# Convolution stage: the inverse transform in three tiles of 120 rows, one more rounded sequence, and a finer order of steps

## The chip, the cores and the metric

The kernel runs on one core of one Trainium2 chip. The metric is device time in microseconds, from one launch; the kernel before takes 2923.79 us (median of 3 runs, 2923.07 to 2927.09).

## What is computed

The reference chains three layers over 2 sequences of 12480 positions and 128 channels. This change touches the first one alone:

```
h_filt = (maximum(pos_emb @ w1, 0) @ w2) * window
Uf = rfft(x * v, n=2 * S);  Hf = rfft(h_filt, n=2 * S)
y = irfft(Uf * Hf, n=2 * S)[:, :S]
out = x * y
```

Two feed-forward layers follow: 128 to 2048 to 128, first with an ELU, then with h * cos(h).

## The kernel before, in words

The program has three stages. First the filter taps are made (lines 203 to 308). Then the convolution runs (lines 310 to 477). Last come the two feed-forward layers (from line 480), which this change leaves alone; they read the convolution's result `xt_d` from DRAM.

The convolution is a Fourier transform written as matmuls. A position is split into a (98 rows) and b (128 columns), and the transform has 90 frequencies along a (`NF`) and 128 along b (`NB`). The 128 channels go in 32 chunks of 4 (`DC` = 4, `NCH` = 32). Each chunk has three inputs: the data sequences k = 0 and k = 1, and the filter taps, k = 2. These are the steps for a chunk c:

- `prod` (line 318): u = x * v on POOL. Each chunk's x and v come in by two DMAs of SP (`load`, line 193).
- Stage A, `st_a` (line 335), for k = 0, 1, 2: the transform over a in plain fp32 into the PSUM tile `ps_a`, 4 matmuls of 180 columns. DVE multiplies by the twiddles (`za`, `zb`, line 345), POOL adds (`z_t`, line 348). For k = 2 ACT also makes the rounded copy `zh` and POOL the remainder `zl` (line 359).
- Stage B, `st_b` (line 362): the transform over b into `ps_b`, 360 columns (4 channels of 90). For k = 0 and 1 it is 4 matmuls in fp32. For k = 2 it is 12 matmuls in the rounded type fp32r: high times high, low times high, high times low. For k = 2 ACT copies the result out as `hr` and `hi_f` (lines 381 to 383). For k = 0 and 1 DVE multiplies by those (`ya` and in place in `ps_b`, lines 389 and 390) and adds (`y_t`, line 392); ACT rounds (`yh`), POOL takes the remainder (`yl`, line 332).
- Stage C, `st_c` (line 397), k = 0 and 1: the inverse over b into `ps_c`. The rows are one channel's 90 frequencies; for each of 4 channels there are 6 rounded matmuls of 256 columns, 24 in all. DVE multiplies by twiddles (`wa`, `wb`, line 412, 90 x 1024), POOL adds (`w_t`, line 419).
- Stage D, `st_d` (line 422), k = 0 and 1: the inverse over a into `ps_d`, 2 fp32 matmuls of 512 columns. DVE multiplies by x (`at`, line 428), SP writes the result to `xt_d` (line 429).

`ps_a`, `ps_b`, `ps_c` and `ps_d` have one buffer each. So a stage may write its tile again only when DVE or ACT has emptied it.

Between these steps the weights of the feed-forward layers are decoded from double words, in small pieces (`top` and `low`, lines 457 to 461; the DVE rows `size`, `mag`, `pw` and the POOL rows `lf`, `full`, `lo` belong to it).

The order is written by hand. The schedule is manual, so each engine runs its instructions in the order in which the Python code emits them. The tuple `steps` (line 465) holds one period: each entry is a whole stage with the number of chunks that it lags and its k. It is run 34 times (line 469).

Of the kernel before, what the change touches and what calls it, by code (L numbers as in the profile page):

```python
# [19 lines left out]
NA = 98  # L20
NB = 128
# [7 lines left out]
NCH = D // DC  # L29
T = 480  # L30
# [22 lines left out]
def tables():  # L53
# [27 lines left out]
def hyena_moe_kernel(ctx: ExitStack, tc: tile.TileContext, x, v, pe, w1, w2,  # L81
# [92 lines left out]
    with tc.manual_schedule():  # L174
        nc.vector.memset(below, BELOW)
        with ExitStack() as cs:
# [4 lines left out]
            ti_t = const.tile([NF, 2, 4 * NB], F32, name="ti_t")  # L181
# [128 lines left out]
            with ExitStack() as vs:  # L310
# [5 lines left out]
                us, zz, yy, hh, ww = {}, {}, {}, {}, {}  # L316

                def prod(c, k):
                    if c < NCH:
                        us[c, k] = p2.tile([NA, DC, NB], F32, name="u_t")  # L320
                        nc.gpsimd.tensor_tensor(us[c, k], xs[c][:, k], vv[c][:, k], op=ALU.mult)
# [7 lines left out]
                def lo_y(c, k):  # L329
                    y, yh = yy[c, k]  # L330
                    yl = p2.tile([NB, 2, DC * NF], F32R, name="yl")
                    nc.gpsimd.tensor_tensor(yl, y, yh.bitcast(F32), op=ALU.subtract)
                    yy[c, k] = (yh, yl)

                def st_a(c, k):
                    ps = pa.tile([NB, 2, 512], F32, name="ps_a")
# [4 lines left out]
                    n = 4 * NF  # L341
                    t1 = p2.tile([NB, 2 * n], F32, name="za")
                    t2 = p2.tile([NB, 2 * n], F32, name="zb")
                    for q, t in ((0, t1), (1, t2)):
                        nc.vector.tensor_tensor(bank2(t), ps[:, :, 0:n],  # L345
                                                tw_t[:, q:q + 1].to_broadcast([NB, 2, n]), op=ALU.mult)
                    z = p2.tile([NB, 2, DC * NF], F32, name="z_t")
                    nc.gpsimd.tensor_tensor(z.rearrange("p r (s k) -> p r s k", s=DC),  # L348
                                            parts(t1, NF), parts(t2, NF)[:, ::-1], op=ALU.add)
                    if k == 2:  # L350
                        zh = skewed(p1, [NB, 2, DC * NF], F32R, SKEW, name="zh")
                        copy_r(zh, z)
# [9 lines left out]
                def st_b(c, k):  # L362
                    ps = pa.tile([NB, 2, 512], F32, name="ps_b")
# [4 lines left out]
                    for r in range(2):  # L368
                        for j, (sl, q) in enumerate(prs[r]):
                            if k == 2:  # L370
                                zh, zl = z
                                mm = ((dft_h, zh), (dft_l, zh), (dft_h, zl))
                            else:
                                mm = ((dft_t, z),)
                            for i, (a, b) in enumerate(mm):
                                nc.tensor.matmul(ps[:, r, 0:n], a[:, sl], b[:, q], start=j == 0 and i == 0,  # L376
                                                 stop=j == 1 and i == len(mm) - 1)
# [15 lines left out]
                    yh = skewed(p2, [NB, 2, n], F32R, SKEW, name="yh")  # L393
                    copy_r(yh, y)
                    yy[c, k] = (y, yh)

                def st_c(c, k):
                    yh, yl = yy.pop((c, k))
                    last = c == NCH - 1
                    ps = pa.tile([NF, 2, 512], F32, name="ps_c", tag="ps_a" if last and k else "ps_c")  # L400
                    n = 2 * NB
                    for s in range(DC):
                        sl = slice(s * NF, (s + 1) * NF)
                        o = ps[:, s // 2, (s % 2) * n:(s % 2 + 1) * n]
                        mm = [(yt[:, r, sl], th[:, (1 - r) * NB:(3 - r) * NB])
                              for r in range(2) for yt, th in ((yh, dft_h), (yh, dft_l), (yl, dft_h))]
                        for j, (a, b) in enumerate(mm):
                            nc.tensor.matmul(o, a, b, start=j == 0, stop=j == 5)  # L408
                    t1 = p1.tile([NF, DC * n], F32, name="wa")
                    t2 = skewed(p1, [NF, DC * n], F32, SKEW, name="wb")  # L410
                    for q, t in ((0, t1), (1, t2)):
                        nc.vector.tensor_tensor(bank2(t), ps, ti_t[:, q:q + 1].to_broadcast([NF, 2, 512]), op=ALU.mult)
                    w = p2.tile([NF, 2, DC, NB], F32, name="w_t")
                    p, q = parts(t1, NB), parts(t2, NB)[:, ::-1]
                    if last:
                        nc.gpsimd.tensor_tensor(w[:, 0], p[:, 0], q[:, 0], op=ALU.add)
                        nc.vector.tensor_tensor(w[:, 1], p[:, 1], q[:, 1], op=ALU.add)
                    else:
                        nc.gpsimd.tensor_tensor(w, p, q, op=ALU.add)
                    ww[c, k] = w  # L420

                def st_d(c, k):
                    w = ww.pop((c, k))
                    ps = pd.tile([NA, DC, NB], F32, name="ps_d")
                    for r in range(2):
                        nc.tensor.matmul(ps, g_t[:, r * NA:(r + 1) * NA], w[:, r], start=r == 0, stop=r == 1)  # L426
                    at = p2.tile([NA, DC, NB], F32, name="at")
                    nc.vector.tensor_tensor(at, ps, xs[c][:, k], op=ALU.mult)
# [26 lines left out]
                bits, rest = bits_of_all(), parts_of_all()  # L455

                def low(c, k):
                    next(rest, None)

                def top(c, k):  # L460
                    next(bits, None)

                next(bits)
                prod(0, 0)
                steps = ((st_b, 1, 0), (prod, 0, 1), (top, 0, 0), (lo_y, 1, 0), (low, 0, 0), (top, 0, 1), (st_a, 0, 2),
                         (st_c, 2, 1), (top, 0, 2), (lo_z, 0, 2), (low, 0, 1), (st_b, 1, 1), (st_a, 0, 0), (lo_y, 1, 1),
                         (st_d, 2, 0), (low, 0, 2), (st_c, 1, 0), (prod, -1, 0), (st_b, 0, 2), (st_a, 0, 1), (top, 0, 3),
                         (st_d, 2, 1))
                for p in range(NCH + 2):
                    for f, back, k in steps:  # L470
                        if 0 <= p - back < NCH or f in (top, low):
                            f(p - back, k)
                    load(p + 2)
# [223 lines left out]
```

## Time and profile before

| | |
|---|---|
| median of 3 runs | 2923.79 us |
| profiled execution, first to last instruction | 2922.3 us |
| PE busy over the span | 2888.7 us (99%) |
| POOL busy | 2632.8 us (90%) |
| DVE busy | 2497.0 us (85%) |
| ACT busy | 2146.6 us (73%) |

The page gives no time for the profiled execution other than its span; the span is 1.5 us below the median of the runs. The trace is read here in microseconds from the span's first instruction. The convolution stage runs from about 51 to 692. "PE" is the matmul itself and "PEld" the load of its stationary operand, which goes on beside it. A matmul's recorded duration includes its way through the array and overlaps the next one, so lengths on PE are taken from start to start. An fp32 matmul is two PE instructions in the trace, a rounded one is one. "SPq" and "ACTq" are DMA issues on those queues.

### The profile page before, as it was taken

Reading aid. Unit: us, or ns where it says so; the run is one execution under the profiler, and the core shown is the slowest. Engines: PE = TensorE matmul, PEld = TensorE weight load, DVE = VectorE, ACT = ScalarE, POOL = GpSimd, SP = SyncE. Lnnn points to the kernel's source line nnn. Section 1 sums busy time; section 2 is a strip of 40 time slices with the busy share of each in tenths; the row PEclk is TensorE's granted clock in tenths of the full one; section 3 lists DMA queues with packets and bytes.
Section 4 is the critical chain, followed back from the end, with each engine's and each line's share of the span. In section 5 each row is a group of like instructions: output and inputs, shape, how many; then the busy total and the mean of one; then the engine's idle time right before and its main releaser. Section 6 shows DMA issues by size and latency. Waiting matters only on the chain.

```text
span 2922.3 us, 40341 instructions
## 1 busy us (share of the span) xinstructions
PE 2888.7 (99%) x13580; PEld 2393.3 (82%) x13580; DVE 2497.0 (85%) x3241; ACT 2146.6 (73%) x3332; POOL 2632.8 (90%) x1908
## 2 busy tenths in 40 slices
PE   8999999998999999999999999999999999999999
PEld 6878787886888888888888887888888888888887
DVE  5888888887998998899899998888888888888887
ACT  3322323224988898888888888888888888888887
POOL 4888888886999999999999998999999999999998
PEclk9999999998999999999999999999999999999999
DMA  3333333333000000000000001000000000000000
GB/s 105 90 81 88 97 89 86 88 83 97 14 11 14 11 12 14 14 11 11 14 11 14 11 11 60 11 14 11 14 11 14 11 11 14 11 14 11 13 12 14
DMA packets 83104, 96.82 MB, mean 33 GB/s; under 512 B 6106, under 2 KB 68088, under 8 KB 82898
## 3 DMA queue, kind: packets, MB, share of 16 engines
q1 hardware_dynamic: 77072, 88.20, 10.6%
q10 hardware_dynamic: 5826, 6.04, 0.7%
q8 instruction: 109, 1.79, 0.3%
q14 instruction: 97, 0.79, 0.1%
HBM read 59.94 MB, written 34.28 MB: 32 GB/s over the span
## 4 chain that ended last, share of the span: by engine, by line
PE 92%; ACT 3%; DVE 2%; issue 2%; POOL 1%; DMA 0%; ACTq 0%; POOLq 0%; DVEq 0%
PE h_ps L545 35%; PE o_ps L614 34%; PE ps_b L376 8%; PE ps_c L408 6%; PE ps_a L340 4%; PE ps_d L426 4%; ACT e L582 1%; DVE e L575 1%; DVE e L584 1%; ACT e L573 1%; PE h_ps L277 1%; ACT gh L97 1%; ACT ot L622 1%; PE w_ps L218 0%; PE r_ps L259 0%
## 5 line engine op out<-in xcount | busy, mean ns | idle before, releaser
L106 POOL TENSOR_TENSOR gl<-e,gh 128x960 fp32r<-128x960 f32 x780 | 1463.7, 1888 | 88.6 <-ACT gh L97 45.3
L545 PE MATMUL h_ps<-xh,w 128*128 128x480 f32 x3328 | 1022.3, 388 | 15.5 <-DVE e L562 5.5
L614 PE MATMUL o_ps<-gh,w 128*128 128x480 f32 x3120 | 933.0, 380 | 0.0
L545 PEld LDWEIGHTS h_ps<-xh,w 128*128 128x128 f32 x3328 | 623.0, 189 | 150.5 <-issue 26.6
L614 PEld LDWEIGHTS o_ps<-gh,w 128*128 128x128 f32 x3120 | 586.8, 188 | 92.9 <-POOL gh L105 0.2
L575 DVE SCALAR_TENSOR_TENSOR e<-e,h_ps 128x960 f32<-128x960 int32 x416 | 479.9, 1154 | 193.1 <-ACT e L573 67.0
L545 PE MATMUL h_ps<-xl,w 128*128 128x480 f32 x1664 | 634.6, 381 | 0.0
L560 DVE SCALAR_TENSOR_TENSOR e<-e,t_ps 128x480 f32<-128x480 f32 x832 | 539.6, 652 | 108.8 <-ACT t_ps L558 87.7
L614 PE MATMUL o_ps<-gl,w 128*128 128x480 f32 x1560 | 594.3, 381 | 2.0 <-POOL gl L106 2.0
L556 ACT ACTIVATE e<-h_ps 128x480 f32<-128x480 f32 x832 | 475.5, 572 | 141.6 <-PE h_ps L545 106.9
L573 ACT ACTIVATE e<-h_ps 128x960 int32<-128x960 f32 x416 | 404.1, 971 | 149.8 <-PE h_ps L545 148.0
L105 POOL TENSOR_SCALAR gh<-e 128x960 fp32r<-128x960 f32 x468 | 466.8, 998 | 42.1 <-DVE e L562 24.1
L558 ACT ACTIVATE t_ps<-h_ps 128x480 f32<-128x480 f32 x832 | 479.4, 576 | 0.0
L562 DVE SCALAR_TENSOR_TENSOR e<-e,h_ps 128x480 f32<-128x480 f32 x780 | 472.3, 647 | 0.0
L582 ACT ACTIVATE e<-e,half_pi 128x960 f32<-128x960 f32 x416 | 453.9, 1091 | 0.3 <-DVE e L575 0.3
L584 DVE TENSOR_TENSOR e<-e,h_ps 128x960 f32<-128x960 f32 x390 | 447.2, 1147 | 1.3 <-ACT e L582 1.2
L545 PEld LDWEIGHTS h_ps<-xl,w 128*128 128x128 f32 x1664 | 314.3, 189 | 52.3 <-POOL xl L106 0.6
L614 PEld LDWEIGHTS o_ps<-gl,w 128*128 128x128 f32 x1560 | 293.7, 188 | 50.6 <-POOL gl L106 3.2
L97 ACT ACTIVATE gh<-e 128x960 fp32r<-128x960 f32 x312 | 312.4, 1001 | 0.0
L376 PE MATMUL ps_b<-z_t,dft_t 128*128 128x360 f32 x512 | 165.7, 466 | 2.1 <-DVE y_t L392 1.7
L348 POOL TENSOR_TENSOR z_t<-za,zb 128x720 f32<-128x720 f32 x96 | 141.1, 1470 | 26.3 <-DVE zb L345 26.3
L408 PE MATMUL ps_c<-dft_h,yh 128*90 128x256 f32 x512 | 160.4, 313 | 0.0
(90 smaller groups left out, 3066.7 us busy)
## 6 DMA issues: line engine op xcount, KB each, us to landing
x_t<-in_x SPq DMA_DIRECT2D x32, 392.0 KB
v_t<-in_v SPq DMA_DIRECT2D x32, 392.0 KB
xt_d<-at SPq DMA_DIRECT2D x64, 196.0 KB
out<-ot SPq DMA_DIRECT2D x52, 240.0 KB
x_in<-xt_d SPq DMA_DIRECT2D x50, 240.0 KB
raw<-in_wi SPq DMA_DIRECT2D x16, 256.0 KB
w_d<-hi SPq DMA_DIRECT2D x32, 128.0 KB
w_d<-lo SPq DMA_DIRECT2D x32, 128.0 KB
```

The costliest lines, as they stand in the source:

```text
L105: ENG[plan[0]].tensor_scalar(hi, full, 1.0, 0.0, op0=ALU.mult, op1=ALU.add)
L106: ENG[plan[1]].tensor_tensor(lo, full, hi.bitcast(F32), op=ALU.subtract)
L545: nc.tensor.matmul(h[:, 0:T], a, b, start=k == 0, stop=k == 2)
L556: nc.scalar.activation(u[:, e], hs[e][:, 0:T], AF.Exp)
L558: nc.scalar.activation(ts[e][:, 0:T], hs[e][:, 0:T], AF.Tanh, scale=0.5)
L560: nc.vector.scalar_tensor_tensor(u[:, e], u[:, e], 1.0, ts[e][:, 0:T], op0=ALU.add, op1=ALU.mult)
L562: nc.vector.scalar_tensor_tensor(gt[:, e], u[:, e], 0.0, hs[e][:, 0:T], op0=ALU.min, op1=ALU.max)
L573: nc.scalar.activation(kq, hv, AF.Copy, scale=1.0 / TWO_PI, bias=0.25)
L575: nc.vector.scalar_tensor_tensor(rr, kq, -TWO_PI, hv, op0=ALU.mult, op1=ALU.add)
L582: nc.scalar.activation(rr, rr, AF.Sin, bias=half_pi)
L584: nc.vector.tensor_tensor(gt, rr, hv, op=ALU.mult)
L614: nc.tensor.matmul(o, a, b[:, e], start=f == 0 and k == 0, stop=f == NFT - 1 and k == len(mm) - 1)
```

## The change

**Three tiles.** Stage C now works on 3 tiles of 120 rows (`NM` = 120, `NT` = 3), each with the 90 frequencies of one channel and 30 frequencies of the fourth. For that, DVE's add that writes `y_t` stores its columns in another order and is two instructions, one for three channels and one for the fourth. DVE's two multiplies and POOL's add behind stage C have 120 x 768 elements in place of 90 x 1024. Stage D needs the fourth channel on 90 rows again: three DMAs on SP's queue move 30 rows each from `w_t` to a new tile `v_w`. Stage D is then 2 matmuls of 384 columns from `w_t` and 2 of 128 columns from `v_w`.

**Rounded passes.** Stage B for k = 1 takes the rounded form that k = 2 has: ACT makes `zh`, POOL makes `zl`, and 12 rounded matmuls replace 4 in fp32. In both, the 8 products that need only `zh` are emitted ahead of the 4 that need `zl`.

**Order.** The stages are cut into steps (matmuls, evacuation, add, rounding), and a new list of 44 steps is one period. The filter's stage A runs one chunk ahead, and stage B follows stage A within the period. The loads of x and v are issued at the end of the period, as before. The table `ti_t` grows from 90 x 1024 to 120 x 1536 words.

```diff
+NT = 3
+NM = DC * NF // NT
...
+                    if len(z) == 1:
+                        groups = (((dft_t, z[0]),),)
+                    else:
+                        groups = (((dft_h, z[0]), (dft_l, z[0])), ((dft_h, z[1]),))
...
-                nc.vector.tensor_tensor(y, t1, pv[:, ::-1], op=ALU.add)
...
+                    for o, a, b, e in ((slice(0, NF), 0, m, NT), (slice(NF, NM), m, n, NT)):
+                        nc.vector.tensor_tensor(yv[:, :, :, o], t1[:, :, a:b].rearrange("p r (i k) -> p r i k", i=e),
+                                                q[:, :, a:b].rearrange("p r (i k) -> p r i k", i=e), op=ALU.add)
...
-                    for s in range(DC):
-                        sl = slice(s * NF, (s + 1) * NF)
-                        o = ps[:, s // 2, (s % 2) * n:(s % 2 + 1) * n]
+                    for i in range(NT):
+                        sl = slice(i * NM, (i + 1) * NM)
...
+                    v = p2.tile([NF, 2, NB], F32, name="v_w")
+                    m = NM - NF
+                    for i in range(NT):
+                        nc.sync.dma_start(v[i * m:(i + 1) * m], w[NF:NM, i])
+                    ww[c, k] = (w, v)
...
+                    for o, rhs in ((ps[:, 0:NT], w[0:NF]), (ps[:, NT:DC], v.rearrange("p (i r) b -> p i r b", i=1))):
+                        for r in range(2):
+                            nc.tensor.matmul(o, g_t[:, r * NA:(r + 1) * NA], rhs[:, :, r], start=r == 0, stop=r == 1)
...
-                steps = ((st_b, 1, 0), (prod, 0, 1), (top, 0, 0), (lo_y, 1, 0), (low, 0, 0), (top, 0, 1), (st_a, 0, 2),
...
-                for p in range(NCH + 2):
...
+                steps = """
+                    t c21 l10 A00 D20 a00 y11 C10 A01 w21 L02 Y11 z00 d20 B02 t a01 o c10 o u-10
+                    D21 o z01 l11 h02 w10 t t B00 A-12 d21 y00 H01 u-11 C11 L01 B01 Y00 a-12 z-12
+                    x-20 H-12
+""".split()
```

In the new list a capital A, B, C or D is a stage's matmuls, the small letter its evacuation (h and y for stage B), z and w POOL's adds, H and Y the roundings on ACT, L and l the remainders on POOL, t and o the decoding, u the product, x the loads. The first number is the lag in chunks, the last digit is k. So PE's order in a period is A00 D20 C10 A01 B02 D21 B00 A-12 C11 B01.

On PE, in the middle of a period, before the change: the end of the filter's stage B, then stages A, D, B, A and the start of C.

```order
L376 MATMUL ps_b<-zl,dft_h 128x360
L340 MATMUL ps_a<-fa_t,u_t 128x180 x4
L426 MATMUL ps_d<-w_t,g_t 98x512 x2
L376 MATMUL ps_b<-z_t,dft_t 128x360 x4
L340 MATMUL ps_a<-fa_t,h_all 128x180 x4
L408 MATMUL ps_c<-dft_h,yh 90x256
```

And with the change:

```order
L385 MATMUL ps_b<-zl_1401,dft_h 128x360 x4
L463 MATMUL ps_d<-w_t,g_t 98x384 x2
L463 MATMUL ps_d<-v_w,g_t 98x128 x2
L385 MATMUL ps_b<-z_t,dft_t 128x360 x4
L342 MATMUL ps_a<-fa_t,h_all 128x180 x4
L432 MATMUL ps_c<-dft_h,yh 120x256
```

Stage A for a data sequence no longer stands between the filter's stage B and stage D, and stage D ends with two matmuls that read the moved rows.

On DVE, around the step that empties `ps_b`, before the change:

```order
L428 TENSOR_TENSOR at<-ps_d,x_t 98x512
L389 TENSOR_TENSOR ya<-ps_b,hr 128x720
L390 TENSOR_TENSOR ps_b<-ps_b,hi_f 128x2x360
L392 TENSOR_TENSOR y_t<-ya,ps_b 128x720
L139 TENSOR_SCALAR size<-ps_w 128x256
L143 SCALAR_TENSOR_TENSOR ps_w<-ps_w,size 128x256
L345 TENSOR_TENSOR za<-ps_a,tw_t 128x720
L345 TENSOR_TENSOR zb<-ps_a,tw_t 128x720
L412 TENSOR_TENSOR wa<-ps_c,ti_t 90x1024
L412 TENSOR_TENSOR wb<-ps_c,ti_t 90x1024
```

And with the change:

```order
L467 TENSOR_TENSOR at<-ps_d,x_t 98x512
L402 TENSOR_TENSOR ya<-ps_b,hr 128x720
L403 TENSOR_TENSOR ps_b<-ps_b,hi_f 128x2x360
L408 TENSOR_TENSOR y_t<-ya,ps_b 128x6x90
L408 TENSOR_TENSOR y_t<-ya,ps_b 128x6x30
L349 TENSOR_TENSOR za<-ps_a,tw_t 128x720
L349 TENSOR_TENSOR zb<-ps_a,tw_t 128x720
L144 TENSOR_SCALAR size<-ps_w 128x256
L440 TENSOR_TENSOR wa<-ps_c,ti_t 120x768
L440 TENSOR_TENSOR wb<-ps_c,ti_t 120x768
```

The add is two instructions, and the filter's `za`, `zb` stand directly behind it.

On SP's queue, one period before the change:

```order
L429 DMA xt_d<-at 98x4x128
L164 DMA w_d<-hi 128x256
L120 DMA raw<-in_wo 128x2x128
L429 DMA xt_d<-at 98x4x128
L198 DMA x_t<-in_x 98x2x512
L199 DMA v_t<-in_v 98x2x512
L170 DMA w_d<-lo 128x256
```

And with the change:

```order
L455 DMA v_w<-w_t 30x256 x3
L468 DMA xt_d<-at 98x4x128
L175 DMA w_d<-lo 128x256
L169 DMA w_d<-hi 128x256
L455 DMA v_w<-w_t 30x256 x3
L125 DMA raw<-in_wo 128x2x128
L468 DMA xt_d<-at 98x4x128
L203 DMA x_t<-in_x 98x2x512
L204 DMA v_t<-in_v 98x2x512
```

Seven DMAs a period become thirteen; the first three copies now stand behind the previous period's loads of x and v, the other three ahead of this period's.

## Rows read from the trace of the kernel before

**Rows 1.** The page: its first line, and busy time with share of the span.

```profile
span 2922.3 us, 40341 instructions
PE 2888.7 (99%) x13580; PEld 2393.3 (82%) x13580; DVE 2497.0 (85%) x3241; ACT 2146.6 (73%) x3332; POOL 2632.8 (90%) x1908
```

**Rows 2.** By stretch: length, busy PE, PEld, DVE, ACT, POOL, clock, DMA share, GB/s.

```profile
317.44:650.47 333.03, 333.03 (x1837) 266.59 (x1836) 293.94 (x374) 99.42 (x204) 279.66 (x222) 1.00 0.33 89
650.00:700.00 50.00, 44.28 (x219) 31.94 (x217) 33.54 (x41) 7.63 (x15) 27.84 (x23) 0.91 0.41 125
...
324.00:326.00 2.00, 2.00 (x12) 1.47 (x11) 2.00 (x3) 1.14 (x2) 1.65 (x2) 1.00 0.00 0
```

**Rows 3.** The page: the chain of waits that ended last, by engine.

```profile
PE 92%; ACT 3%; DVE 2%; issue 2%; POOL 1%; DMA 0%; ACTq 0%; POOLq 0%; DVEq 0%
```

**Rows 4.** Timeline of PE, one period, then 17 periods on: start, duration, instructions.

```profile
301.91 2.58 PE L376 MATMUL ps_b<-z_t,dft_t 128*128 128x360 f32 x8
304.33 1.39 PE L340 MATMUL ps_a<-fa_t,u_t 98*128 98x180 f32 x8
305.55 1.88 PE L426 MATMUL ps_d<-w_t,g_t 90*98 90x512 f32 x4
...
310.09 0.33 PE L376 MATMUL ps_b<-zh,dft_h 128*128 128x360 f32 x1
...
312.08 1.38 PE L340 MATMUL ps_a<-fa_t,u_t 98*128 98x180 f32 x8
313.30 1.88 PE L426 MATMUL ps_d<-w_t,g_t 90*98 90x512 f32 x4
315.02 2.59 PE L376 MATMUL ps_b<-z_t,dft_t 128*128 128x360 f32 x8
317.44 1.39 PE L340 MATMUL ps_a<-fa_t,h_all 98*128 98x180 f32 x8
...
321.49 1.37 PE L376 MATMUL ps_b<-z_t,dft_t 128*128 128x360 f32 x4
...
650.47 1.39 PE L340 MATMUL ps_a<-fa_t,h_all 98*128 98x180 f32 x8
```

**Rows 5.** Timeline of PEld in the filter stage: two loads of 128 columns.

```profile
41.78 0.30 PEld L259 LDWEIGHTS r_ps<-pe_t,w_t 128*128 128x128 f32 x2
```

**Rows 6.** Groups by line and form, 100 to 650 us: count, busy us, mean ns.

```profile
L348 POOL TENSOR_TENSOR z_t<-za,zb 128x720 f32<-128x720 f32 x85 | 124.9, 1470 | 16.8 <-DVE zb L345 16.8
L419 POOL TENSOR_TENSOR w_t<-wa,wb 90x1024 f32<-90x1024 f32 x57 | 113.7, 1995 | 10.0 <-DVE wb L412 10.0
...
L376 PEld LDWEIGHTS ps_b<-z_t,dft_t 128*128 128x128 f32 x454 | 84.2, 190 | 52.7 <-issue 14.1
...
L345 DVE TENSOR_TENSOR zb<-ps_a,tw_t 128x720 f32<-128x720 f32 x84 | 75.4, 897 | 0.0
L412 DVE TENSOR_TENSOR wb<-ps_c,ti_t 90x1024 f32<-90x1024 f32 x56 | 67.8, 1210 | 0.0
L359 POOL TENSOR_TENSOR zl<-z_t,zh 128x720 fp32r<-128x720 f32 x28 | 40.7, 1455 | 0.0
L428 DVE TENSOR_TENSOR at<-ps_d,x_t 98x512 f32<-98x512 f32 x57 | 38.7, 679 | 0.0
```

**Rows 7.** Timeline of DVE in that period: the steps that empty `ps_b`.

```profile
317.70 0.91 DVE L389 TENSOR_TENSOR ya<-ps_b,hr 128x720 f32<-128x720 f32 x1 [1.55 <-issue]
...
319.46 0.90 DVE L392 TENSOR_TENSOR y_t<-ya,ps_b 128x720 f32<-128x720 f32 x1
```

**Rows 8.** Timeline of ACT in that period: the last copy out of `ps_b`.

```profile
313.00 0.48 ACT L383 ACTIVATE hi_f<-ps_b 128x360 f32<-128x360 f32 x1
```

**Rows 9.** Timeline of DMA issues: x of a chunk, and a read-back with its reader.

```profile
316.56 0.84 SPq L198 DMA_DIRECT2D x_t<-in_x  x1
...
691.05 0.34 ACTq L523 DMA_DIRECT2D x_in<-xt_d  x1
...
693.76 0.59 POOL L105 TENSOR_SCALAR xh<-x_in 128x480 fp32r<-128x480 f32 x1 [4.77 <-DMA x_in<-xt_d]
```

More of the change, by code (lines that the diff above doesn't have):

```diff
@@ L315, in hyena_moe_kernel @@
                 bank = vs.enter_context(tc.tile_pool(name="bank", bufs=1, space=PSUM))
[L316 to L321, printed above, removed]
+                us, pas, za_, zz, pbs, hh, yy, pcs, wab, ww, pds = ({} for _ in range(11))
+                PS = {"a": "ps_a", "b": "ps_b", "c": "ps_c"}
                 def bank2(t):
@@ L346, in st_a, with add_z @@
                                                 tw_t[:, q:q + 1].to_broadcast([NB, 2, n]), op=ALU.mult)
+                    za_[c, k] = t1, t2
+                def add_z(c, k, at):
+                    t1, t2 = za_.pop((c, k))
                     z = p2.tile([NB, 2, DC * NF], F32, name="z_t")
@@ L367, in st_b @@
                     z = zz.pop((c, k))
[L368 to L377, printed above, removed]
@@ new lines, in mm_b, with out_h @@
+                    for i, group in enumerate(groups):
+                        for r in range(2):
+                            mm = [(a[:, sl], b[:, q]) for sl, q in prs[r] for a, b in group]
+                            for j, (a, b) in enumerate(mm):
+                                nc.tensor.matmul(ps[:, r, 0:n], a, b, start=i == j == 0,
+                                                 stop=i == len(groups) - 1 and j == len(mm) - 1)
+                def out_h(c, k, at):
+                    ps, n = pbs.pop((c, k)), DC * NF
+                    hr = p2.tile([NB, 1, n], F32, name="hr")
+                    hi = p2.tile([NB, 2, n], F32, name="hi_f")
+                    nc.scalar.activation(hr[:, 0], ps[:, 0, 0:n], AF.Copy)
+                    nc.scalar.activation(hi[:, 0], ps[:, 1, 0:n], AF.Copy)
+                    nc.scalar.activation(hi[:, 1], ps[:, 1, 0:n], AF.Copy, scale=-1.0)
+                    hh[c] = (hr, hi)
@@ L386, in st_b, with mul_y @@
+                def mul_y(c, k, at):
                     hr, hi = hh[c]
+                    ps, n = pbs.pop((c, k)), DC * NF
                     t1 = p1.tile([NB, 2, n], F32, name="ya")
@@ L414, in st_c, with out_c @@
-                    p, q = parts(t1, NB), parts(t2, NB)[:, ::-1]
-                    if last:
+                            nc.tensor.matmul(ps[:, i * n:(i + 1) * n], a, b, start=j == 0, stop=j == 5)
+                    pcs[c, k] = ps
+                def out_c(c, k, at):
+                    ps, n = pcs.pop((c, k)), NT * 2 * NB
+                    t1 = p1.tile([NM, n], F32, name="wa")
+                    t2 = skewed(p1, [NM, n], F32, SKEW, name="wb")
+                    for q, t in ((0, t1), (1, t2)):
+                        nc.vector.tensor_tensor(t, ps[:, 0:n], ti_t[:, q], op=ALU.mult)
+                    wab[c, k] = t1, t2
@@ L416, in st_c, with add_w @@
+                def add_w(c, k, at):
+                    p, q = (t.rearrange("p (i r k) -> p i r k", i=NT, r=2) for t in wab.pop((c, k)))
+                    q = q[:, :, ::-1]
+                    w = p2.tile([NM, NT, 2, NB], F32, name="w_t")
+                    if c == NCH - 1:
                         nc.gpsimd.tensor_tensor(w[:, 0], p[:, 0], q[:, 0], op=ALU.add)
-                        nc.vector.tensor_tensor(w[:, 1], p[:, 1], q[:, 1], op=ALU.add)
+                        nc.vector.tensor_tensor(w[:, 1:NT], p[:, 1:NT], q[:, 1:NT], op=ALU.add)
@@ L418, in st_c @@
                     else:
                         nc.gpsimd.tensor_tensor(w, p, q, op=ALU.add)
[L420 to L426, printed above, removed]
+                    v = p2.tile([NF, 2, NB], F32, name="v_w")
+                    m = NM - NF
@@ L455, in hyena_moe_kernel, with low, top, fetch @@
                 bits, rest = bits_of_all(), parts_of_all()
-                def low(c, k):
+                next(bits)
+                def low(c, k, at):
                     next(rest, None)
-                def top(c, k):
+                def top(c, k, at):
                     next(bits, None)
-                next(bits)
-                prod(0, 0)
-                steps = ((st_b, 1, 0), (prod, 0, 1), (top, 0, 0), (lo_y, 1, 0), (low, 0, 0), (top, 0, 1), (st_a, 0, 2),
-                         (st_c, 2, 1), (top, 0, 2), (lo_z, 0, 2), (low, 0, 1), (st_b, 1, 1), (st_a, 0, 0), (lo_y, 1, 1),
-                         (st_d, 2, 0), (low, 0, 2), (st_c, 1, 0), (prod, -1, 0), (st_b, 0, 2), (st_a, 0, 1), (top, 0, 3),
-                         (st_d, 2, 1))
-                for p in range(NCH + 2):
[L470 to L473, printed above, removed]
+                def fetch(c, k, at):
+                    if c not in xs:
+                        load(c)
+                FN = dict(u=prod, A=mm_a, a=out_a, z=add_z, H=hi_z, L=lo_z, B=mm_b, h=out_h, y=mul_y, Y=hi_y, l=lo_y,
+                          C=mm_c, c=out_c, w=add_w, D=mm_d, d=out_d, t=top, o=low, x=fetch)
+                def step(name, c, k, at=""):
+                    if name in "to" or 0 <= c < NCH:
+                        FN[name](c, k, at)
+                steps = """
[3 more added lines that the diff above has]
+""".split()
+                back = lambda s: (s[0], int(s[1:-1]) if len(s) > 1 else 0, int(s[-1]) if len(s) > 1 else 0)
+                for p in range(-2, NCH + 4):
+                    for f, b, k in map(back, steps):
+                        if f in "to" and not 0 <= p < NCH + 2:
+                            continue
+                        step(f, p - b, k)
                 for _ in bits:
```

85 lines of the change are left out of this document (44 added, 41 removed).

## The prediction

> **What bounds the kernel now.** I began with the page's busy times: PE is busy 99% of 2922.3 us, POOL 90%, DVE 85% [rows 1]. A mean over stages says little about one stage, so I cut out 17 whole periods of the convolution, 317.44 to 650.47 [rows 2]. There PE is busy all of 333.03 us at full clock (1.00), and the others are not: per period DVE works 293.94 / 17 = 17.29 us, POOL 279.66 / 17 = 16.45, ACT 5.85. The chain of waits agrees: 92% of it lies on PE [rows 3].
>
> A busy PE may still hide gaps, since its durations overlap. So I read one period start to start [rows 4]: stage B in fp32 2.42 (301.91 to 304.33, again from 315.02), stage A 1.22, stage D 1.72 (313.30 to 315.02), the rounded stage B 1.99 (310.09 to 312.08). Stage C is what is left: 310.09 - 305.55 - 1.72 = 2.82, and 321.49 - 317.44 - 1.22 = 2.83. The sum is 2 x 2.42 + 3 x 1.22 + 2 x 1.72 + 1.99 + 2.82 + 2.83 = 19.58. The period itself is 333.03 / 17 = 19.59. Nothing is left between the stages: PE's own work sets the pace, and an engine beside it costs nothing until it takes longer than PE.
>
> **Part by part, per period.**
>
> *Stage C.* 24 matmuls take 2.82, or 0.118 each. With 18 of the same 256 columns it is 2.12, twice a period: -1.41. The loads grow from 90 to 120 columns; two loads of 128 columns stand 0.30 - 0.19 = 0.11 apart [rows 5, 6], so one still fits under its matmul. The bound on the bad side is stage A's pace, 1.22 / 8 = 0.152 with loads of 128 columns: 18 x 0.152 = 2.74, a gain of 0.16 in all. I take 0.118, as the load row is the nearer one.
>
> *Stage B, k = 1.* 2.42 in fp32 becomes the 1.99 that the rounded one shows [rows 4]: -0.43. The Trainium skill (FP8 and Floating Point Precision, TensorE Precision Notes) says that true fp32 makes 4 passes through the array; taken alone that makes three passes an estimated 1.82, a gain of 0.60, and the forecast 5 us lower. The rows differ from it: a rounded matmul of 360 columns takes 1.99 / 12 = 0.166, a quarter of an fp32 one 2.42 / 16 = 0.151. The measured gain stands.
>
> *Stage D.* The columns stay 512, split 384 and 128. An instruction of 512 takes 1.72 / 4 = 0.43, so by columns nothing changes. The 128-column instructions would take 0.107, just under the 0.11 between loads; at stage A's 0.152 they would cost 4 x 0.045 = 0.18, twice. I take 0; the bound is +0.36.
>
> *PE in sum.* -1.84: a period of 17.74, over 32 chunks -58.9 us.
>
> *DVE.* Four multiplies behind stage C go from 1024 to 768 elements. Between 720 at 0.897 and 1024 at 1.210 [rows 6] that is 0.95, so -0.26 x 4 = -1.04. The add that writes `y_t` is cut in two; a straight line through 512 at 0.679 and 720 at 0.897 leaves some 0.14 without any element, of which instructions in a row overlap a part (317.70 to 319.46 is two of them in 1.76 [rows 7]). I take +0.1, twice. DVE comes to 16.45, under PE's 17.74.
>
> *POOL.* `w_t` goes from 1.995 to some 1.55 (between 1.470 at 720 and 1.995 at 1024), -0.88; a second `zl` adds 1.46 [rows 6]. POOL comes to 17.03: hidden, but with only 0.7 to spare. ACT gets one more rounding of under 1 us and stays below 7.
>
> *The copies.* Six DMAs a period. Nothing in this trace copies within SBUF. The nearest row is a read-back of 240 KB: its reader starts 693.76 - 691.05 - 0.34 = 2.4 after the issue [rows 9]. With three issues of 0.34 a copy takes 3.4. What hides it: for k = 1, from the end of stage C to the moved part of stage D, PE has B, A, D, C, A, B and D's first part, 1.99 + 1.22 + 1.72 + 2.12 + 1.22 + 1.99 + 1.29 = 11.6. DVE's queue and POOL's `yl` and `w_t` take some 5.9 of it ahead of the copy, so 5.7 is left. For k = 0 the same walk leaves 6.3. The copies for k = 1 stand behind x and v of the period before on SP's queue. Those are issued from 316.56 and no traffic is left at 324.00 [rows 2, 9], so under 7.5 in all; POOL's `w_t` comes some 6 after them, which can add 1.5. 3.4 + 1.5 is still under 5.7: nothing.
>
> *The single buffers.* The new order has two tight places. `ps_b` after stage B of k = 0: PE covers with A and C, 1.22 + 2.12 = 3.34. DVE's first multiply starts 0.26 after PE's next stage (317.70 against 317.44), the add ends at 320.36 [rows 4, 7], and with its second instruction that is 3.02. `ps_b` after the filter's stage B: cover is D, 1.72; ACT's last copy ends at 313.48, 1.40 behind PE's next stage at 312.08 [rows 4, 8]. Both leave some 0.3, and the way back to PE takes, by the 0.26 of the way out, nearly all. I take 0.06 a period, 2 us; bounds 0 and 0.4 a period, 13 us.
>
> *Fill and drain.* 34 periods are passed either way, and between 650 and 700 PE is busy only 44.28 of 50 at a clock of 0.91 [rows 2]. In the drain no stage covers the last chunk's copies. Bounds 0 and two copies, 7; I take 3, about one, since the first feed-forward block reads k = 0 alone.
>
> **The sum.** 2922.3 - 58.9 + 2 + 3 = 2868.4 for a profiled execution. The median of the runs is 1.5 above the span, so 2870 us. With the bounds (both waits at 0; or D's 11.5, the buffers' 13 and the drain's 7 all at their worst) this case reaches from 2865 to 2896, most of it below 2880.
>
> **The rivals.**
>
> *The waits eat part of it.* POOL at 17.03 of 17.74 and both `ps_b` places on edge: a half microsecond lost per period is 16 us, 2886. For it speaks that DVE, POOL and PE now run within 8% of each other with one buffer per stage; against it, that 19.58 of 19.59 was reached before with the same buffers.
>
> *The copies land one after another: slower.* If three copies don't overlap, they take 3 x 2.4 + 0.3 = 7.5. Stage D then waits 1.8 for k = 1 and 1.2 for k = 0, 3.0 against the 1.84 gained: +1.16 a period, +37 us, and with fill, drain and the 1.5 it is 2966. It decides from (1.84 + 5.7 + 6.3) / 2 = 6.9 us per copy on. Against it: x and v, nearly nine times these bytes (2 x 392 KB against 90), are through in under 7.5 together [rows 2, 9]. If they overlap in part and take 6.2, only k = 1 waits, 0.5 a period: 2886. The Trainium skill (SBUF — State Buffer, The DMA setup-cost knee; Can I just issue two DMAs to hit both halves?) gives a DMA some 2 us apart from its bytes, and says that two at a time serialise; read together that is an estimated 6.2 for three. [...]
>
> *The loads set stage C's pace.* At 0.152 the gain is 0.16 + 0.43 = 0.59, 19 us: 2910. The 0.11 of rows 5 and 6 speaks against it.
>
> *The change doesn't do what it says:* POOL's or DVE's waits hold the period at the old 19.6, and the time stays within 0.2%, about what a measurement here can tell from no change (3 runs spread by 0.14%). With 16.45 and 17.03 us of work against 19.59 this needs 2.5 us of new waits.
>
> **How the numbers follow.** The forecast gets 0.72, the waits 0.13, copies at 6.2 us 0.03, the loads 0.05, copies at 7.5 us 0.05, no change 0.02. Faster is the first four, 0.93. The range holds the forecast's case to near its bad end and the partial losses: 2862 to 2893; the low end is 3 under the best sum, as the pieces are read to 0.01 us and 32 chunks multiply that.
>
> **What would show it.** Right: periods of 17.7 to 17.9 us, PE busy throughout them; 36 stage C matmuls per period 0.118 apart; POOL busy some 96%; no wait of stage D on a DMA. Wrong: PE idle ahead of stage B on DVE or ACT (the buffers), or stage D's 128-column matmuls waiting on the DMA (the copies), or stage C's matmuls further apart (the loads).

## The result, and the profile after

The changed kernel takes 2879.3 us, median of 4 runs (2878.04 to 2881.25), against 2924.68 for the kernel before on the same chip: a ratio of 0.9847, with a 95% interval of 0.9834 to 0.986. The profiled execution has a span of 2877.7 us, 44.6 less than before [rows 1]. Forecast were 2870 us with a range of 2862 to 2893: the direction and the range hold, the gain is 9 us smaller than said.

The page, first line and busy times:

```profile
span 2877.7 us, 40773 instructions
PE 2834.5 (98%) x13580; PEld 2393.0 (83%) x13580; DVE 2465.2 (86%) x3305; ACT 2167.7 (75%) x3364; POOL 2647.5 (92%) x1940
```

PE loses 54.2 us of busy time, about what was forecast for the whole, but the span only 44.6: some 10 us of PE work was replaced by waits. To see where, I cut both traces at the same four events: the filter's first stage A, its third, its 32nd and last, and the first activation of the feed-forward part. This is busy time by stretch, columns as in rows 2; first the kernel after, then the kernel before:

```profile
50.93:87.21 36.28, 26.42 (x118) 22.34 (x119) 19.85 (x30) 11.61 (x25) 22.28 (x19) 0.81 0.15 45
87.21:602.59 515.38, 515.38 (x3134) 452.15 (x3133) 471.88 (x696) 189.40 (x377) 489.89 (x407) 1.00 0.40 109
602.59:654.54 51.95, 41.57 (x219) 33.05 (x217) 31.33 (x45) 7.79 (x14) 28.85 (x26) 0.87 0.45 134
```

```profile
50.97:82.36 31.39, 25.58 (x121) 21.28 (x122) 20.51 (x28) 10.29 (x23) 19.26 (x16) 0.84 0.26 76
82.36:650.47 568.11, 568.11 (x3133) 454.78 (x3132) 501.43 (x638) 169.91 (x349) 479.02 (x380) 1.00 0.32 88
650.47:699.36 48.89, 43.27 (x217) 31.69 (x215) 33.54 (x41) 6.99 (x14) 27.37 (x23) 0.91 0.40 122
```

The middle line of each is 29 whole periods: 568.11 / 29 = 19.59 became 515.38 / 29 = 17.77, with PE busy throughout. That gives 52.7 us. The first line is the fill, in which the first chunks come in, the last the drain, in which the last ones run out: the fill grew by 4.9 us, the drain by 3.1. PE stands still in them for 36.28 - 26.42 = 9.9 and 51.95 - 41.57 = 10.4 us, before for 5.8 and 5.6. After the first activation both kernels take the same, 2222.9 us before and 2223.2 now. So 52.7 - 4.9 - 3.1 = 44.7: the steady part does what was forecast, and the ends give back.

One period of PE in the changed kernel, without stage C and the rounded stages B (timeline: start, duration; it answers to rows 4):

```profile
584.82 1.39 PE L342 MATMUL ps_a<-fa_t,h_all 98*128 98x180 f32 x8
...
590.17 1.38 PE L342 MATMUL ps_a<-fa_t,u_t 98*128 98x180 f32 x8
591.39 1.46 PE L463 MATMUL ps_d<-w_t,g_t 90*98 90x384 f32 x4
592.68 0.60 PE L463 MATMUL ps_d<-v_w,g_t 90*98 90x128 f32 x4
...
595.24 1.38 PE L342 MATMUL ps_a<-fa_t,u_t 98*128 98x180 f32 x8
...
598.44 1.45 PE L463 MATMUL ps_d<-w_t,g_t 90*98 90x384 f32 x4
599.73 0.60 PE L463 MATMUL ps_d<-v_w,g_t 90*98 90x128 f32 x4
600.16 2.59 PE L385 MATMUL ps_b<-z_t,dft_t 128*128 128x360 f32 x8
602.59 1.39 PE L342 MATMUL ps_a<-fa_t,h_all 98*128 98x180 f32 x8
```

One fp32 stage B is left (600.16 to 602.59), stage D in two pieces still ends 1.72 after its start (598.44 to 600.16), and none of these rows shows a wait. From the end of stage D (592.68 + 0.43) to 595.24 stage C's 18 matmuls take 2.13, or 0.118 each. The groups by line and form between 100 and 600 us answer to rows 6:

```profile
L451 POOL TENSOR_TENSOR w_t<-wa,wb 120x768 f32<-120x768 f32 x56 | 86.5, 1544 | 0.0
L440 DVE TENSOR_TENSOR wb<-ps_c,ti_t 120x768 f32<-120x768 f32 x57 | 54.1, 949 | 0.0
L463 PEld LDWEIGHTS ps_d<-v_w,g_t 90*98 90x98 f32 x228 | 31.1, 165 | 18.2 <-issue 18.0 <-DMA v_w<-w_t 0.2
```

`w_t` at 1544 ns and the multiply at 949 stand where the prediction put them (1.55 and 0.95). The last row says that stage D waited for a copy for 0.2 us in 500: in the steady part the copies are hidden. In the drain they are not. PE there, and the two queues (timeline):

```profile
629.42 1.46 PE L463 MATMUL ps_d<-w_t,g_t 90*98 90x384 f32 x4
632.62 0.65 PE L463 MATMUL ps_d<-v_w,g_t 90*98 90x128 f32 x4 [1.75 <-DMA v_w<-w_t]
635.24 1.45 PE L463 MATMUL ps_d<-w_t,g_t 90*98 90x384 f32 x4
640.37 1.17 PE L463 MATMUL ps_d<-v_w,g_t 90*98 90x128 f32 x4 [3.67 <-DMA v_w<-w_t]
642.41 2.85 PE L463 MATMUL ps_d<-w_t,g_t 90*98 90x384 f32 x4 [0.88 <-DVE at L467]
```

```profile
627.27 2.49 SPq L455 DMA_DIRECT2D v_w<-w_t  x3
...
632.92 4.37 SPq L455 DMA_DIRECT2D v_w<-w_t  x3
```

```profile
629.47 10.46 ACTq L559 DMA_DIRECT2D w<-w_d  x7
...
644.64 0.34 ACTq L574 DMA_DIRECT2D x_in<-xt_d  x1
...
647.06 6.77 ACTq L559 DMA_DIRECT2D w<-w_d  x5
```

Stage D of chunk 31's k = 0, on which the feed-forward part waits, stands 3.67 us for its copies; these took 4.37 us to issue alone, and the seven weight loads on ACT's queue 10.46. `x_in` is the read-back of the convolution's result; the first activation follows it on ACT behind further weight loads. Before, the same seven took 5.60 (ACT's queue in the kernel before):

```profile
679.11 5.60 ACTq L508 DMA_DIRECT2D w<-w_d  x7
```

### The profile page after: what moved, and what is told of

It is laid out like the page before. It is cut to its first block, busy times and chain, and to the rows that moved or that the text cites. A ratio compares the mean times of both kernels' runs of the same rounds, so it can differ in the third digit from the quotient of the medians.

```text
span 2877.7 us, 40773 instructions
## 1 busy us (share of the span) xinstructions
PE 2834.5 (98%) x13580; PEld 2393.0 (83%) x13580; DVE 2465.2 (86%) x3305; ACT 2167.7 (75%) x3364; POOL 2647.5 (92%) x1940
## 4 chain that ended last, share of the span: by engine, by line
PE 90%; ACT 3%; DVE 3%; issue 2%; POOL 1%; DMA 1%; ACTq 0%; SPq 0%; POOLq 0%; DVEq 0%
PE h_ps L596 36%; PE o_ps L665 35%; PE ps_b L385 7%; PE ps_c L432 4%; PE ps_a L342 4%; PE ps_d L463 4%; ACT e L633 1%; DVE e L626 1%; DVE e L635 1%; ACT e L624 1%; ACT gh L102 1%; PE h_ps L282 1%; ACT ot L673 1%; PE w_ps L223 0%; PE r_ps L264 0%
## 5 line engine op out<-in xcount | busy, mean ns | idle before, releaser
L102 ACT ACTIVATE yh<-y_t 128x720 fp32r<-128x720 f32 x64 | 51.7, 807 | 225.0 <-DVE y_t L408 220.6
L432 PE MATMUL ps_c<-dft_h,yh 128*120 128x256 f32 x384 | 114.7, 299 | 0.0
```

## The experiments

The theory: in the period PE's own work is the bound, as forecast; what is missing was lost in the fill and the drain, to the new order and to the copies. The rivals: another engine already sets part of the period; the copies sit closer to their cover than forecast; the drain is long through something else, such as the weights' arrival.

**The parts undone one at a time.** First the rounding of k = 1:

```diff
-D21 o z01 l11 h02 w10 t t B00 A-12 d21 y00 H01 u-11 C11 L01 B01 Y00 a-12 z-12
+D21 o z01 l11 h02 w10 t t B00 A-12 d21 y00 u-11 C11 B01 Y00 a-12 z-12
```

> One part undone: stage B of k = 1 goes back to one fp32 product per pair (no rounding on ACT, no second zl on POOL); tiles, copies and order stay. Theory (PE's own work sets the period): its stage B takes 2.42 instead of 1.99, the period goes from the changed kernel's 17.77 to 18.20 us, the span from 2877.7 to some 2891 (32 x 0.43 = 13.8). Rival (POOL, at 95% of the period in the changed kernel, sets it): POOL loses 1.46 us a period, and the period stays at 17.8 or falls, span 2878 or less.

Span 2889.7, median 2890.98. From the filter's third stage A to its last, by stretch:

```profile
85.95:614.13 528.18, 528.18 (x3017) 439.06 (x3016) 471.69 (x696) 169.26 (x348) 448.79 (x378) 1.00 0.39 106
```

528.18 / 29 = 18.21: +0.44, as the theory said, with PE busy throughout. POOL works 448.79 / 29 = 15.5 us a period instead of 489.89 / 29 = 16.9, and the period got longer: POOL does not set it. Then the tiles:

```diff
-NT = 3
+NT = 4
-for o, a, b, e in ((slice(0, NF), 0, m, NT), (slice(NF, NM), m, n, NT)):
+for o, a, b, e in ((slice(0, NF), 0, m, NT),):
-v = p2.tile([NF, 2, NB], F32, name="v_w")
-m = NM - NF
-for i in range(NT):
-    nc.sync.dma_start(v[i * m:(i + 1) * m], w[NF:NM, i])
```

(and stage D as one product of 512 columns again.)

> The other part undone: stages C and D on four tiles of 90 rows, no channel moved, no copies; rounded stage B of k = 1 and the new order stay. Theory: 24 matmuls at 0.118 make stage C 2.83 again, the period is 17.77 + 2 x 0.71 = 19.18 us; 64 stages C make 45.1 us, which would give a span of 2922.8, but the drain has no copies to wait for and gives back some 5 to 7 us: 2916 to 2918. Rival (the copies cost nothing in the drain; the order of the last steps makes it long): 2922 to 2924. Second rival (the three tiles gave less, since another engine sets the period): period under 19.0.

Span 2915.5, median 2917.23.

```profile
85.54:641.27 555.73, 555.73 (x3249) 468.39 (x3248) 501.74 (x638) 189.27 (x378) 517.09 (x407) 1.00 0.32 91
```

555.73 / 29 = 19.16: three tiles are worth 1.39 a period. The span lies just below the band that the theory gave and well below 2922, so the drain does get shorter when there are no copies.

**The order alone.** Both edits together leave nothing of the change but the order of the steps:

> The new order of steps alone: four tiles, no copies, stage B of k = 1 in fp32. Theory (PE's own work sets the period, and the new order has longer ends): period 19.17 + 0.43 = 19.60, as in the kernel before (19.59). With four tiles the time from the last filter stage A to the first activation left 16.1 us without PE work, against 11.5 before: +4.6 here; the fill +3.6 against before. Span 2922.3 + 8 = 2930. Rival (the order costs nothing at the ends, what the ends lost came from the rounding and the copies): span 2921 to 2924.

Span 2930.4, median 2930.23, a ratio to before of 1.0017 (1.0008 to 1.0027). By stretch, cut at the same events:

```profile
50.48:87.17 36.69, 27.43 (x120) 22.81 (x121) 20.34 (x28) 10.23 (x23) 21.02 (x18) 0.81 0.18 52
87.17:655.47 568.30, 568.30 (x3134) 454.85 (x3132) 501.71 (x638) 169.06 (x348) 477.30 (x378) 1.00 0.32 89
655.47:706.00 50.53, 42.37 (x213) 30.40 (x212) 34.09 (x41) 6.97 (x13) 27.29 (x23) 0.90 0.38 111
```

The period is that of before (19.60 against 19.59); the fill is 5.3 us longer, the drain 1.6. Taken alone, the order costs 6.9 us at the ends in these two profiled executions; by the medians it is 5 us, with an interval from 2 to 8. All of the fill's growth is its doing: all eleven kernels here that have the new order and the single buffers show a fill of 35.5 to 36.7 us, against 31.4 before. What it is good for, to hide the copies and the second rounding, cannot be seen with both taken out.

**The copies in the drain.** For the last three stages D the nine copies are left out, and with them one channel's part of these chunks:

```diff
+if c == NCH - 1 or c == NCH - 2 and k == 1:
+    v = w[0:NF, 0]
+else:
     for i in range(NT):
         nc.sync.dma_start(v[i * m:(i + 1) * m], w[NF:NM, i])
```

> The changed kernel without the last nine copies (k = 1 of the last chunk but one, and both of the last chunk): stage D reads rows of `w_t` that are already there in place of the moved channel's, so this channel's output of these chunks is not computed. Theory (the drain waits on the copies: PE stood 1.75 and 3.67 us ahead of stage D's last part, and the weight loads on ACT's queue took 10.5 us for seven issues, 5.6 before): stage D of the last chunk's k = 0 comes some 5 us earlier, the first activation of the feed-forward part at 649 to 650 instead of 654.5, span 2872 to 2873. Rival (the arrival of the feed-forward weights, or the order of the last steps, sets its start): span within 1.5 us of 2877.7.

Span 2870.2, median 2871.64. From the filter's last stage A to the first activation, and ACT's queue:

```profile
600.96:646.90 45.94, 36.48 (x211) 30.07 (x210) 31.14 (x45) 7.80 (x15) 28.89 (x26) 0.89 0.45 131
```

```profile
627.87 6.21 ACTq L562 DMA_DIRECT2D w<-w_d  x7
...
639.88 0.34 ACTq L577 DMA_DIRECT2D x_in<-xt_d  x1
...
642.30 3.68 ACTq L562 DMA_DIRECT2D w<-w_d  x5
```

The drain is 6.0 us shorter than the changed kernel's 51.95, and the seven weight loads issue in 6.21 us instead of 10.46. Only part of the 6.0 comes through stage D: the read-back is issued 38.92 us after the last filter stage A instead of 42.05, 3.1 sooner. The other 2.9 lie behind it, where the first activation follows in 7.02 us instead of 9.90; the five weight loads there take 3.68 us to issue and not 6.77. So the 6.0 go with the copies, but about half of it by way of the weight loads and not of stage D. The other 1.5 us of the span come from the start, where this run's first periods came early, as they do in some executions; I count 6.0.

**Why they are slow there.** Two kernels move DMAs to POOL's queue, which issues none in the drain of the changed kernel (POOL itself is not idle there: it works 28.85 of the 51.95 us). One moves the first eight weight loads:

```diff
-layers[0].load(nc.scalar, wh, q)
+layers[0].load(nc.scalar if wh else nc.gpsimd, wh, q)
```

> The changed kernel with the first eight weight loads of the feed-forward part issued from POOL's queue instead of ACT's. Theory (in the drain the copies wait for these loads, and the loads for the copies, since the two queues' transfers share their semaphores): the three issues for k = 0 of the last chunk take 2.5 us again instead of 4.4, its stage D waits 1.8 us less, ACT issues without holes, and the span falls by 2 to 3.5 us to 2874 to 2876. Rival (the copies only share the DMA engines with the loads' bytes): the issues stay at 4 us or over and the span within 1 us of 2877.7.

Span 2875.8, median 2877.14: -1.9, at the edge of what was expected. SP's queue and stage D of chunk 31's k = 0:

```profile
631.78 2.56 SPq L455 DMA_DIRECT2D v_w<-w_t  x3
```

```profile
635.74 0.65 PE L463 MATMUL ps_d<-v_w,g_t 90*98 90x128 f32 x4 [1.54 <-DMA v_w<-w_t]
```

The three issues are back from 4.37 to 2.56, and the wait from 3.67 to 1.54. Stage D starts 1.4 us after the third issue has ended, in the changed kernel 3.1 (637.29 to 640.37). On POOL's queue the eight loads come only behind these copies:

```profile
635.99 5.95 POOL L559 DMA_DIRECT2D w<-w_d  x8
```

So it is the weight loads under way that slow the copies in the drain, and 1.54 us of the wait remain without them, as PE has too little work there to cover the copy. How the loads do it is not told apart, through their transfers or through the signalling of an end. In the changed kernel the chain of waits puts the third issue behind the landing of an earlier write-out of SP's own queue:

```profile
629.86 5.63 DMA xt_d<-at
```

The 1.8 us that the drain gains here do not come through stage D: the read-back is issued 43.28 us after the last filter stage A, 42.05 in the changed kernel, but the first activation follows it in 6.86 us instead of 9.90. The other kernel moves one copy of three, for the last three stages D:

```diff
-nc.sync.dma_start(v[i * m:(i + 1) * m], w[NF:NM, i])
+q = nc.gpsimd if end and i == 0 else nc.sync
+q.dma_start(v[i * m:(i + 1) * m], w[NF:NM, i])
```

> The changed kernel with one of the three copies issued from POOL's queue, for the last three stages D alone; POOL is idle there. Theory (the three issues in a row on SP, 2.5 us and 4.4 in the drain, make the copy long): stage D follows the end of `w_t` 0.8 to 1.5 us sooner, and the span falls by 1 to 2.5 us. Rival (the landing, not the issue, makes it long, or a copy from POOL's queue lands later than one from SP's): no gain, span within 1 us of 2877.7 or above.

Span 2877.3, median 2878.02: no gain in the span. Stage D of chunk 31's k = 0 does follow the end of `w_t` sooner, by 5.4 us instead of 7.5, and the drain is 1.7 us shorter (50.29), but what comes behind the first activation takes 2225.0 us there instead of 2223.2. Inconclusive.

**How close the copies are to their cover.** One or three more copies, into a tile that nobody reads, ahead of the three (here three):

```diff
+x = p2.tile([NF, 2, NB], F32, name="v_x", bufs=1)
+for i in range(3):
+    nc.sync.dma_start(x[i * m:(i + 1) * m], w[NF:NM, i])
```

> The changed kernel with one more copy of 30 rows, into a tile that nobody reads, issued on SP's queue ahead of the three. Theory A (in the changed kernel's drain stage D follows the end of w_t by 5.4 us, of which 2.5 are the three issues; with cover of 5.75 us for k = 1 and 6.33 for k = 0 only 0.4 is left): the copy then takes 5.4 + 0.83 = 6.2, stage D of k = 1 waits some 0.45 a period, period 18.2, span some 2891. Theory B (the forecast's 3.4 us per copy is right in the steady part): 3.4 + 0.83 = 4.2 is still covered, period 17.77, span 2878.

> As the run with one more copy, with three more ahead of the three. Theory A (5.4 us per copy, cover 5.75 and 6.33): 5.4 + 2.5 = 7.9, stage D waits some 2.1 for k = 1 and 1.5 for k = 0, period 21.4, span some 2985 (30 periods x 3.6). Theory B (3.4 us): 3.4 + 2.5 = 5.9, 0.15 of wait for k = 1 alone, period 17.9, span under 2885.

Spans 2885.6 and 2935.9, medians 2885.84 and 2939.36: both between the two theories. With three more, a period from the filter's fourth stage A to its last takes 19.74 us on average. SP's queue and stage D there:

```profile
272.99 2.44 SPq L458 DMA_DIRECT2D v_w<-w_t  x3
```

```profile
276.81 0.65 PE L466 MATMUL ps_d<-v_w,g_t 90*98 90x128 f32 x4 [0.80 <-DMA v_w<-w_t]
```

Where stage D really waits, it mostly starts 1.4 us after the third issue has ended (here 275.43 to 276.81; 1.3 to 2.3 over all of this run's waits). In the changed kernel the third issue ends some 2.55 us after `w_t`, so a copy takes 2.55 + 1.4 = 4.0 us. Its stages D start 5.74 and 6.32 us after `w_t`: some 1.7 and 2.3 us are to spare, and theory A is wrong. The 5.4 us that it took from the drain are a copy beside the weight loads: with these loads behind the copies, on POOL's queue, the same stage D starts 3.9 us after `w_t` (626.09):

```profile
630.03 0.65 PE L463 MATMUL ps_d<-v_w,g_t 90*98 90x128 f32 x4 [0.31 <-DMA v_w<-w_t]
```

One more copy should then cost nothing, yet it costs 8 us in the profiled execution (6.5 by the medians; its four runs reach from 2879.90 to 2887.35). Its waits between 100 and 600 us (engine, waited for: us in total, times, longest):

```profile
POOL u_t L335 <- DMA v_t<-in_v: 17.5, 17, 1.7
...
PEld ps_d L466 <- DMA v_w<-w_t: 7.0, 11, 1.1
...
PEld ps_b L385 <- POOL zl L368: 5.3, 16, 0.4
```

In the changed kernel the first two are 1.0 and 0.2, and the third is not there. POOL stood 17.5 us for v, whose load comes behind the copies and x on SP's queue. POOL, busy 95% of a period, has no time for that: its `zl` comes late, and the rounded stages B stand 5.3 us for it. The stages D, read start to start, are 2.9 us longer in total, as some of them start only 2.9 to 3.1 us after the third issue. Both together are 8.2 of the 8.6 us that the 29 periods grew. The test of this moves v's load to ACT's queue, with the one copy more kept:

```diff
-nc.sync.dma_start(vv[c], v[:, :, c * DC:(c + 1) * DC, :])
+(nc.sync if c < 4 else nc.scalar).dma_start(vv[c], v[:, :, c * DC:(c + 1) * DC, :])
```

> As the run with one more copy ahead of the three (2885.6 us), but from chunk 4 on v is loaded from ACT's queue instead of SP's. Theory (that run lost its 8 us because the copies push the loads of x and v back on SP's queue: POOL's u_t waited for v 4.7 us between 157 and 300, and POOL, 95% busy, cannot make it up): with v off the queue period 17.77 again, span 2877 to 2879. Rival (the longer copy itself makes stage D wait): span stays at 2885 to 2886.

Span 2882.3, median 2884.16. POOL no longer waits for v at all, nor stage B for `zl`, but the period falls only from 18.08 to 17.96 (both over those 28 periods), and stages D wait. One of them, for k = 0, with the two queues' issues before it (timeline):

```profile
143.21 2.46 SPq L458 DMA_DIRECT2D v_w<-w_t  x3
144.19 0.82 ACTq L204 DMA_DIRECT2D v_t<-in_v  x1
149.53 0.65 PE L466 MATMUL ps_d<-v_w,g_t 90*98 90x128 f32 x4 [0.40 <-DMA v_w<-w_t]
```

Read start to start, the stages D are 4.3 us longer in total. Those that wait are nearly all for k = 0, while with v on SP's queue they were nearly all for k = 1. So the edit cured v's lateness, and its load, now issued between the copies for k = 0, probably brought these waits with it. The rows of the run before split its 8.6 us better: 5.3 through v and POOL, 2.9 through copies that landed late. Neither theory holds alone.

**The ends mended.** In the first period, stages write into PSUM buffers that stand empty there:

```diff
+at = {"A0": "b", "A1": "c", "B0": "c"}.get(f + str(k), "") if p == 0 and b == 0 else ""
-step(f, p - b, k)
+step(f, p - b, k, at)
```

> The changed kernel with other PSUM buffers in the first period alone: stage A of k = 0 writes into the one of stage B, stage A of k = 1 and stage B of k = 0 into the one of stage C, which is free then. Theory (the fill is made of waits on single buffers: PE stood 2.06 and 1.91 us for DVE's zb, and stage B of k = 0 at 67.00 behind the filter's hi_f): the first period falls from 18.6 (17.7 to 18.7 in the runs so far) to some 14 to 15, the span to 2873 to 2874. Rival (the fill is one chain through POOL and ACT, whatever the buffers): first two periods as before, span within 1 us of 2877.7.

Span 2872.4, median 2872.14. The first period of the changed kernel, then the first two of this one, by stretch:

```profile
50.93:69.49 18.56, 13.26 (x44) 11.05 (x45) 6.50 (x10) 5.21 (x12) 9.25 (x8) 0.63 0.11 37
```

```profile
51.08:63.45 12.37, 10.58 (x44) 8.85 (x45) 6.31 (x10) 4.62 (x12) 7.39 (x7) 0.86 0.11 40
63.45:82.33 18.88, 14.45 (x75) 12.80 (x74) 13.45 (x20) 7.21 (x14) 14.89 (x13) 0.91 0.22 62
```

The first period takes 12.4 us instead of 18.6, the second 18.9 instead of 17.7; both together 31.25, as short as before the change. So the single buffers made the fill's 5 us. Of these, 3.6 are waits (PE stands still for 6.2 us in place of 9.9), and 1.4 are PE's own work, which is shorter because the first period has a granted clock of 0.86 and no longer 0.63. The second edit puts the last three stages C and D on four tiles of 90 rows again, with the rows of the table that both tilings have in common:

```diff
+def four(c, k):
+    return c == NCH - 1 or c == NCH - 2 and k == 1
...
+g = NF if four(c, k) else NM
-for i in range(NT):
-    sl = slice(i * NM, (i + 1) * NM)
+for i in range(DC * NF // g):
+    sl = slice(i * g, (i + 1) * g)
```

> The changed kernel with the last three stages C and D (k = 1 of chunk 30, both of chunk 31) on four tiles of 90 rows and without copies, the whole output computed. Theory (the copies of these three stages cost 7.5 us: 2877.7 to 2870.2 without them): PE gets 6 matmuls more three times, 2.1 us, partly in holes, and the rest of the 7.5 stays: span 2871 to 2873. Rival (the work put in eats the gain): 2876 or above.

Span 2871.4, median 2873.76; the drain takes 46.49 instead of 51.95. Both together, with the last eight weight loads on SP's queue (`layers[0].load(nc.sync if wh else nc.scalar, wh, q)`):

> Both together, and the last eight weight loads of the feed-forward part on SP's queue, so that ACT's first activation does not stand behind their issue. Theory: the sum of both, -4 and -5.5 us, and 1 us for the queue: span 2866 to 2869, median some 2869, 0.35% under the changed kernel. Rival (what the ends gain is given back at the start of the feed-forward part by the weights' arrival): 2872 or above.

Span 2867.1, median 2868.28, a ratio to before of 0.9804 (0.9789 to 0.9818), against 0.9847 (0.9834 to 0.986) for the changed kernel: the fastest version here. By stretch, fill, period and drain:

```profile
51.09:82.41 31.32, 26.26 (x118) 22.90 (x119) 19.85 (x30) 11.21 (x24) 21.84 (x18) 0.84 0.14 39
82.41:597.82 515.41, 515.41 (x3134) 452.11 (x3133) 471.98 (x696) 189.28 (x377) 489.63 (x407) 1.00 0.39 109
597.82:642.84 45.02, 38.77 (x217) 30.17 (x216) 32.90 (x42) 7.87 (x15) 29.65 (x26) 0.93 0.41 118
```

Fill and drain lose 5.0 and 6.9 us against the changed kernel, and the 29 periods are the same to 0.03 us.

## Why the prediction was right, and which term was too small

- **What bounds the kernel.** "PE's own work sets the pace" held before and after: PE is busy for all of the 515.38 us. The period of 17.77 is the forecast PE sum of 17.74 and 0.03 more.
- **Stage C, -1.41; stage B of k = 1, -0.43.** Undone one by one they are worth 1.39 and 0.44. Stage C's matmuls stand 0.118 us apart with 120 columns loaded, so the rival of the loads falls. The estimate by the Trainium skill (FP8 and Floating Point Precision, TensorE Precision Notes), 0.60 for the rounding, does not agree with the 0.44.
- **Stage D, 0.** The two pieces take 1.72 as the one did.
- **DVE and POOL.** DVE's multiplies and POOL's `w_t` came out within 0.01 us; in all the two work 16.3 and 16.9 us a period, forecast were 16.45 and 17.03. The rivals of the waits and of no change fall with the period, in which PE never stands still.
- **The copies.** 3.4 us against a cover of 5.7 and 6.3 was forecast; it is 4.0 against 5.74 and 6.32. An issue on SP takes 0.8 us and not the 0.34 of ACT's read-back; the row beside it, x on SP's own queue at 0.84 [rows 9], was the nearer one. The landing after it takes 1.4 and not 2.4. The conclusion, nothing lost in the period, stands. Both copy rivals needed 6.2 us or more. For the milder one, the estimate of 6.2 us by the Trainium skill (SBUF — State Buffer, The DMA setup-cost knee; Can I just issue two DMAs to hit both halves?) is not borne out by the 4.0.
- **The single buffers, 0.06 a period.** At most 0.03.
- **Fill and drain, +3 with bounds 0 to 7: the term that was too small.** It was sized as about one copy of the drain. In its place: the forecast credits 32 periods with 1.84 each, the trace has 29 that gain; the three others should have given 5.5 and lost 4.9 + 3.1 instead, so the term is 13.5. The order alone accounts for 6.9 of it (fill 5.3, drain 1.6), which the prediction did not price at all; other buffers in the first period gave 5.0 of that back. "34 periods are passed either way" was read as the same fill, and it is wrong as well: the changed kernel passes its list of 43 steps 38 times (`for p in range(-2, NCH + 4)`), and PE has work in 35 of them. The copies account for 6.0. Stages D stand 1.75 and 3.67 us for them, as they take longer than in the period while the weights of the next part are loaded; about half of the 6.0 shows ahead of the read-back, the rest in the weight loads behind it. By the medians, each against the kernel before on its own chip, the order is 4.8 and the copies 8.4, so the split is good to some 2 us, and the 0.6 that 6.9 and 6.0 leave of the 13.5 stays open. The 10.5 us that this term lacks, less 1 us that the period was better than said, are the 9 us of the miss.
- **The range.** It held by luck in part. The term went beyond its own bound of 7; the range had room because it also allowed 11.5 for stage D and 13 for the buffers, of which hardly anything came.

## What to carry to other kernels

Price the fill and the drain of a pipeline from their own rows: what is free in the period, a copy under cover or a stage moved ahead, costs its full latency where the pipeline is not full yet or no longer, and at the end the next part's loads run beside it. What the ends lose can often be had back at the ends alone, with buffers that stand idle there or the old code for the last pieces, without touching the period. When DMAs are added, count their issues on the queue as well: the next load on that queue, and the engine that waits for it, may have less to spare than the one that reads the copy.

## What the runs showed of the hardware

- Issuing a copy of 30 rows of 1 KB within SBUF held SP's queue 0.8 us (2.49 for three), more than twice a read-back of 240 KB on ACT's queue (0.34) and about as long as a load of x on SP's (0.84) [rows 9]. Three in a row served their reader 4.0 us after their input was there, in the drain beside weight loads 5.4 and 7.5.
- In the drain, issues on two queues were slow together: seven weight loads on ACT took 10.46 us with copies on SP's queue and 6.21 without; three copies on SP took 4.37 with these loads on ACT's queue and 2.56 where the loads came later, on POOL's.
- In the fill PE works in part at the lower of its two clocks, after waits. In the run with other PSUM buffers in the first period, the second period took 18.9 us; most of its first stage C, by stretch:

```profile
71.57:74.97 3.40, 3.40 (x16) 3.40 (x17) 3.31 (x6) 0.36 (x1) 3.39 (x3) 0.53 0.02 5
```

The granted clock is 0.53 there, the level of 1.2 GHz, after PE had waited 1.82 us for DVE ahead of 68.64 and 1.23 for POOL ahead of 71.57. The 16 matmuls stand 3.40 / 16 = 0.21 us apart, against 0.118 in the periods at a clock of 1.00. So the shorter fill moved the lower clock and did not only pay for it: PE's work took 1.3 us more in the second period and 2.7 less in the first.
